# Small matmuls of a chunked recurrent attention laid out as 64x64 tiles in all four places of the array

## The chip, the core and the metric

The kernel runs on one NeuronCore of a Trainium2 chip. A core has five engines that run side by side and meet at semaphores: TensorE (PE) multiplies matrices and writes the results to PSUM; VectorE (DVE), ScalarE (ACT) and GpSimd (POOL) work element by element; SyncE (SP) issues transfers. PSUM has 8 banks of 512 float32 values in each of 128 partitions. The metric is the device time of one execution, in microseconds (us).

## What is computed

An attention with a recurrent state goes through 768 time steps for 4 batches of 8 heads with 40 channels. Its output feeds a mixture of experts with 8 experts.

```python
for t in range(S):
    y[:, :, t] = np.einsum('bhd,bhde->bhe', rt, state)
    Sa = np.einsum('bhde,bhe->bhd', state, at)
    state_decay = state * wt[:, :, None, :] - np.einsum('bhd,bhe->bhde', Sa, bt)
    state = state_decay + np.einsum('bhd,bhe->bhde', vt, kt)
...
for e in range(E):
    h = np.maximum(x @ w1[e], 0.0)
    ye = h @ w2[e]
    out += P[:, e:e + 1] * ye
```

`P` is a gate that is normalized over rows and columns in eight rounds.

## The kernel before

The attention is computed in 12 chunks of 64 time steps (`NCH`, `C`). A chunk is a batch of matrix products, and only a 40x40 state per head passes from chunk to chunk. The 8 heads of a batch are held as 4 pairs (`NP`): the first head of a pair lies on partitions 0 to 39, the second on 64 to 103 (`R2` = 104 partitions in all). Three functions write down the work:

- `prep(c, b)` prepares chunk `c` of batch `b`. It scales the inputs on DVE and POOL (`ab` at L310 is one product per head of the pair, each into its own half of a 128-column tile). `mm_ll` (L325, called `ll` below) multiplies all keys with `ab`, 4 matmuls of 128x128; `mm_kt` (L330, `kt`) transposes. ACT copies the results into a "set" of operands: `SX`, and `BB` (`bb` below).
- `merge(c)` completes the inverse of a triangular 64x64 matrix for each of the 32 heads of a chunk from 16x16 blocks, which DVE has inverted in `inverse`. Its matmuls are small: `mm_ga` (L427), `mm_at` (L433), `mm_tb` (L440, two calls with 32 matmuls each that stream 64 columns: a 32-column block with a block of zeros in front of or behind it), `mm_gb` (L448), `mm_tc` (L455).
- `step(c, b)` is the chain from state to state. `mm_av` (L518, `av`: 4 matmuls of 104x128) is masked by DVE into `f` (L521). `mm_xc` (L529, `xc`: two calls with 4 matmuls each, stationary operand 104 columns) gives `x` in rows 0 to 63 and `c1` in rows 64 to 103 of the same bank; ACT copies both parts of both halves (L534, L536). `mm_pu` (L543, `pu`) multiplies `x` with the inverse, 8 matmuls of 64x64 in two places: rows 0 to 63 into partitions 0 to 63, rows 64 to 127 into 64 to 127. DVE masks it (L546). `mm_c2` (L553, `c2`) is laid out in the same way. DVE adds `c1` to it and gives `ws` (L556). From `ws` come the output `y` (L583, POOL) and the new state `z` (L561, on POOL in chunks 0 to 8, then on DVE), which is transposed (`zt`, L569) for the next chunk. `mm_lp` (L598, `lp`) adds the gate's logits, once per two batches.

All matmuls of this part are in float32; each shows as two rows in the profile, the transposes as one.

The order is not the program's: each operation is put into a `Plan` with an engine, a length, what it depends on, a due time and the buffers that it takes and frees (`Token`). `order()` (L56) replays these lengths and writes the instructions of PE, DVE, ACT, POOL and SP in the order in which they start there. Each engine then runs its list strictly in order. `PACE` (7.5 us a step) sets the due times, `SIZES` the number of buffers; a PSUM token is one of 8 banks.

## Time and profile before

| | us |
|---|---|
| runs of the kernel before: median (lowest, highest) of 3 | 1875.62 (1865.92, 1876.19) |
| the profiled execution: its own time | 1871.58 |
| its span | 1869.6 |
| first to last `pu` matmul (the 48 steps) | 78.4 to 506.2 |
| last matmul of the attention ends, experts begin | about 511 |

The attention is the first quarter of the span and the experts the rest. In the views below a row names an engine, the line of the code, the operation, and the tiles in the form out<-in; `bk` is a PSUM bank. PEld is PE's weight load, which overlaps the matmuls. "issue" as a releaser means that the engine waited for nothing that the profile shows. PEclk is the share of PE's full clock that was granted.

### The profile page before, as it was taken

How to read it: one execution, taken by the hardware profiler on the slowest of the kernel's cores; microseconds unless marked ns; L12 is line 12 of the kernel's file. 1: busy time of each engine (PE TensorE's matmuls, PEld its weight loads, DVE VectorE, ACT ScalarE, POOL GpSimd, SP SyncE). 2: the span in 40 equal slices, each digit the busy share in tenths (PEclk: the TensorE clock that was granted, in tenths of full speed). 3: DMA queues.
4: the chain of work that ended last, by engine and by line, in shares of the span. 5: the costliest groups of instructions: out<-in, count | busy, mean ns of one | idle time of the engine just before them, and what ended most of it. 6: DMA issues, size and time to landing. Idle time of an engine off the chain costs nothing.

```text
span 1869.6 us, 41964 instructions
## 1 busy us (share of the span) xinstructions
PE 1761.5 (94%) x17219; PEld 1715.8 (92%) x17219; DVE 1311.6 (70%) x2278; ACT 877.1 (47%) x1900; POOL 870.7 (47%) x929
## 2 busy tenths in 40 slices
PE   5889999899849999999999999999999999999999
PEld 4778888888738899999999999999999999999999
DVE  8757557364378877686777767886776867767676
ACT  6757667665444434343343434344343434434342
POOL 7645545441175337182653718005371835538170
PEclk9789999888969999999999999999999999999999
DMA  8657666553332111020111102211110201111011
GB/s 184 146 112 153 134 137 150 122 115 72 87 99 60 37 37 56 19 74 19 56 38 38 55 19 74 60 29 38 37 57 18 74 19 56 39 36 65 11 37 43
DMA packets 189572, 126.70 MB, mean 68 GB/s; under 512 B 152261, under 2 KB 169285, under 8 KB 189381
## 3 DMA queue, kind: packets, MB, share of 16 engines
q1 hardware_dynamic: 188901, 123.53, 25.7%
q8 instruction: 135, 2.21, 0.5%
q10 hardware_dynamic: 480, 0.49, 0.1%
q14 instruction: 56, 0.46, 0.1%
HBM read 106.69 MB, written 17.30 MB: 66 GB/s over the span
## 4 chain that ended last, share of the span: by engine, by line
PE 86%; DVE 7%; issue 2%; DMA 2%; ACT 2%; SPq 0%; POOL 0%; DVEq 0%; ACTq 0%
PE op L827 35%; PE p L762 32%; PE bk L529 4%; PE bk L325 2%; PE bk L518 2%; PE bk L543 2%; PE bk L553 2%; PE bk L440 1%; PE bk L455 1%; PE bk L427 1%; PE bk L598 1%; DVE sm L780 1%; DMA xs<-xd 1%; PE bk L448 1%; PE bk L569 1%
## 5 line engine op out<-in xcount | busy, mean ns | idle before, releaser
L762 PE MATMUL p<-xch,wh 128*128 128x384 f32 (+1 forms) x1792 | 605.3, 339 | 30.9 <-ACT xch L736 22.6
L783 ACT ACTIVATE hh<-sm 128x384 fp32r<-128x384 f32 x512 | 269.3, 527 | 722.1 <-DVE sm L780 722.0
L827 PE MATMUL op<-wh,hh 128*128 128x320 f32 x1536 | 477.5, 311 | 2.2 <-ACT hh L783 2.0
L827 PE MATMUL op<-wl,hh 128*128 128x320 f32 x1536 | 475.1, 310 | 0.0
L827 PE MATMUL op<-wh,hl 128*128 128x320 f32 x1536 | 467.3, 310 | 0.3 <-DVE hl L786 0.3
L708 POOL TENSOR_TENSOR wl<-ws,wh 128x640 fp32r<-128x640 f32 x60 | 102.9, 1716 | 605.8 <-ACT wh L706 605.5
L786 DVE SCALAR_TENSOR_TENSOR hl<-sm,hh 128x384 fp32r<-128x384 f32 x512 | 372.4, 761 | 3.2 <-ACT hh L783 2.9
L762 PEld LDWEIGHTS p<-xch,wh 128*128 128x128 f32 (+1 forms) x1792 | 337.5, 188 | 36.2 <-ACT xch L736 22.7
L762 PE MATMUL p<-xcl,wh 128*128 128x384 f32 x896 | 302.8, 338 | 0.6 <-DVE xcl L742 0.6
L762 PE MATMUL p<-xch,wl 128*128 128x384 f32 x896 | 301.9, 337 | 0.0
L827 PEld LDWEIGHTS op<-wh,hh 128*128 128x128 f32 x1536 | 290.4, 189 | 3.6 <-ACT hh L783 3.6
L827 PEld LDWEIGHTS op<-wl,hh 128*128 128x128 f32 x1536 | 291.3, 190 | 0.0
L827 PEld LDWEIGHTS op<-wh,hl 128*128 128x128 f32 x1536 | 287.2, 188 | 0.6 <-DVE hl L786 0.5
L780 DVE TENSOR_TENSOR sm<-p,u 128x384 f32<-128x384 f32 x384 | 235.2, 623 | 8.7
L762 PEld LDWEIGHTS p<-xcl,wh 128*128 128x128 f32 x896 | 168.8, 188 | 1.1 <-DVE xcl L742 1.1
L762 PEld LDWEIGHTS p<-xch,wl 128*128 128x128 f32 x896 | 168.8, 188 | 0.0
L780 DVE TENSOR_TENSOR sm<-p,p 128x384 f32<-128x384 f32 x128 | 71.3, 557 | 129.7 <-PE p L762 75.0
L780 DVE TENSOR_TENSOR p<-p,p 128x384 f32<-128x384 f32 x128 | 71.2, 556 | 102.0 <-PE p L762 101.7
L780 DVE TENSOR_TENSOR u<-p,p 128x384 f32<-128x384 f32 x128 | 70.8, 553 | 58.5 <-PE p L762 57.3
L716 POOL TENSOR_TENSOR wl<-ss,wh 128x512 fp32r<-128x512 f32 x60 | 90.5, 1508 | 35.8 <-ACT wh L713 31.6
L583 POOL TENSOR_TENSOR y<-ws,st 104x256 f32<-104x256 f32 x48 | 39.7, 828 | 122.3 <-DVE ws L556 115.8
L891 DVE SCALAR_TENSOR_TENSOR acc<-op,pmat,acc 128x320 f32<-128x320 f32 x168 | 91.3, 544 | 4.5 <-PE op L827 4.4
(144 smaller groups left out, 2717.8 us busy)
## 6 DMA issues: line engine op xcount, KB each, us to landing
ws<-in_wts_dram SPq DMA_DIRECT2D x60, 832.0 KB
inp<-in_inp_dram SPq DMA_DIRECT2D x48, 450.2 KB
rb<-in_r_dram SPq DMA_DIRECT2D x48, 224.0 KB
ld<-lf SPq DMA_DIRECT2D x48, 128.0 KB
vz<-in_v_dram SPq DMA_DIRECT2D x48, 112.0 KB
f<-in_vt_dram SPq DMA_DIRECT2D x48, 80.0 KB
xd<-y SPq DMA_DIRECT2D x48, 80.0 KB
out_dram<-acc SPq DMA_DIRECT2D x42, 80.0 KB
```

Of the source, the lines that this page charges most:

```text
L325: nc.tensor.matmul(LL()[:, p].rearrange("s h t -> s (h t)"), lhsT=KB()[:, p].rearrange("r k t -> r (k t)"), rhs=AB()[:, p], start=True, st ...
L518: nc.tensor.matmul(AV()[:, p].rearrange("r h t -> r (h t)"), lhsT=VZ()[:, p], rhs=RB()[:, p], start=True, stop=True)
L529: nc.tensor.matmul(wide(b_xc[h])[0:R2, p], lhsT=pp["SX"]()[:, p, h], rhs=F()[:, p, h], start=True, stop=True)
L583: yy.append(P.add("POOL", 0.78, lambda: G.tensor_tensor(out=Y()[0:R2, :, b % 2], in0=WS()[:, :, 0:64], in1=pp["GF"]()[0:R2, :, 64:0:-1], o ...
L708: g.tensor_tensor(out=wl[:, 0:640], in0=raw[:, 256:896], in1=wh[:, 0:640], op=ALU.subtract)
L716: g.tensor_tensor(out=lv[:, 3:7], in0=so[:, :, 0], in1=hv[:, 3:7, 0], op=ALU.subtract)
L762: nc.tensor.matmul(o, lhsT=w_, rhs=x_, start=(j == 0), stop=(j == 3))
L780: eng.tensor_tensor(out=out, in0=x, in1=y, op=ALU.add)
L783: nc.scalar.activation(out=hh[:, f, h], in_=sm[f][:, h], func=AF.Relu)
L786: v.scalar_tensor_tensor(out=hl[:, f, h], in0=sm[f][:, h], scalar=0.0, in1=hh[:, f, h], op0=ALU.max, op1=ALU.subtract)
L827: nc.tensor.matmul(ops[i], lhsT=a[:, h, cs], rhs=w_[:, cw], start=(f == 0 and h == 0 and j == 0), stop=(last and h == 1 and j == 2))
L891: nc.vector.scalar_tensor_tensor(out=acc[:, m], in0=ops[i], scalar=pmat[:, n, e:e + 1], in1=acc[:, m], op0=ALU.mult, op1=ALU.add)
```

## The change

The attention's small matmuls are laid out anew, and the experts' code is untouched.

- PSUM tiles become pairs of banks. A token may take one bank or an aligned pair (`n=2`).
- `ll` and `av` become 16 matmuls of 64x64: the first or second head's rows (row group `h`) times the first or second half of the columns (`k`), in the order of `PLACES`, so that all four 64x64 places of the array are used in turn. Results of row group `h` go to bank `h` of a pair.
- `pu` and `c2` keep 8 matmuls of 64x64 and use four places, row group and column group varying against each other, a bank per row group.
- `xc` is split: `mm_x` gives only `x`, into partitions 0 to 63 for the first head and 64 to 127 for the second, so one ACT copy of 128 partitions takes it out. `mm_c1` gives `c1` into the pair of banks in which `c2` then adds to it (`start=False`). The copies of `c1` and the addition on DVE go.
- `ws` is an ACT copy of 64 columns per head, and `z` is taken by DVE straight from PSUM, in all chunks. The pair is held until both have read it.
- `tb` streams 32 columns in one call of 64 matmuls. ACT writes it out twice: multiplied by a 0/1 column `even` into `tt`, and whole into `r32`, which `tc` streams.
- `ab` is one product for both heads, `r` is loaded without its zero halves (half the bytes), sets go from 15 to 17, `PACE` from 7.5 to 6.0, and the lengths that the plan works with are set anew.

```diff
+    def grab(self, acq):
+            if tok.n == 2:
+                fit = [i for i in f if i % 2 == 0 and i + 1 in f]
+            else:
+                fit = tok.res == "ps" and [i for i in f if i ^ 1 not in f] or f
...
-    bank = many(ps, SZ["ps"], [128, 512], "bk")
+    pair = many(ps, SZ["ps"] // 2, [128, 2, 512], "bk")
...
         def mm_ll():
             for p in range(NP):
-                nc.tensor.matmul(LL()[:, p].rearrange("s h t -> s (h t)"), lhsT=KB()[:, p].rearrange("r k t -> r (k t)"),
-                                 rhs=AB()[:, p], start=True, stop=True)
+                for h, k in PLACES:
+                    nc.tensor.matmul(LL()[halves[k], h, p], lhsT=KB()[halves[h], p, k], rhs=AB()[halves[h], p],
+                                     start=True, stop=True)
...
-        def mm_tb(i):
-            for g in range(8):
-                for k, r in enumerate(quarter):
-                    x = 64 * (i * 8 + g) + (0 if k % 2 else 32)
-                    nc.tensor.matmul(B(b_tb[i], 8, 64)[r, g], lhsT=gt16[r, i * 8 + g], rhs=d16[r, x:x + 64],
-                                     start=True, stop=True)
+        def mm_tb():
+            for g in range(16):
+                for r in quarter:
+                    nc.tensor.matmul(B(b_tb, 16, 32)[r, g], lhsT=gt16[r, g], rhs=d16[r, g], start=True, stop=True)
...
         def mm_av():
             for p in range(NP):
-                nc.tensor.matmul(AV()[:, p].rearrange("r h t -> r (h t)"), lhsT=VZ()[:, p], rhs=RB()[:, p],
-                                 start=True, stop=True)
+                for h, k in PLACES:
+                    x = (slice(0, 64), slice(64, R2))[k]
+                    nc.tensor.matmul(AV()[x, h, p], lhsT=VZ()[halves[h], p, x], rhs=RB()[halves[h], p],
+                                     start=True, stop=True)
...
-                    nc.tensor.matmul(wide(b_xc[h])[0:R2, p], lhsT=pp["SX"]()[:, p, h], rhs=F()[:, p, h],
+        def mm_x():
+            for p in range(NP):
+                for h in range(2):
+                    nc.tensor.matmul(X()[halves[h], p ^ h], lhsT=pp["SX"]()[:, p, h, 0:64], rhs=F()[:, p, h],
                                      start=True, stop=True)
+        def mm_c1():
+            for p in range(NP):
+                for h in range(2):
+                    o = (2 * p + h) * 104 + 64
+                    nc.tensor.matmul(CP()[halves[h], p % 2, p // 2], lhsT=pp["ST"]()[:, o:o + 64], rhs=F()[:, p, h],
+                                     start=p < 2, stop=False)
+        p2 = P.add("PE", 0.74, mm_x, [v1, s0, l_t] + pp["sx"], acq=[b_x, t_x1], rel=[t_f])
+        ax = P.add("ACT", 0.52, lambda: A.copy(out=X1(), in_=X()), [p2], rel=[b_x])
+        pc = P.add("PE", 0.74, mm_c1, [p2] + pp["bb"], acq=[b_c], rel=[t_f])
...
         def mm_pu():
-            for p in range(NP):
-                for h in halves:
-                    nc.tensor.matmul(wide(b_pu)[h, p], lhsT=tt_b[t_tt.slot][h, b * NP + p], rhs=X1()[h, p],
-                                     start=True, stop=True)
+            for a in range(NP):
+                for h in range(2):
+                    nc.tensor.matmul(PU()[halves[(h + a) % 2], h, a // 2], lhsT=tt_b[t_tt.slot][halves[h], b * NP + (a ^ h)],
+                                     rhs=X1()[halves[h], a], start=True, stop=True)
...
         def mm_c2():
-            for p in range(NP):
-                for h in halves:
-                    nc.tensor.matmul(wide(b_c2)[h, p], lhsT=pp["BB"]()[h, p * 40:p * 40 + 64], rhs=PM()[h, p],
-                                     start=True, stop=True)
+            for a in range(NP):
+                for h in range(2):
+                    e, o = (h + a) % 2, (a // 2 * 2 + h) * 40
+                    nc.tensor.matmul(CP()[halves[h], e, a // 2], lhsT=pp["BB"]()[halves[e], o:o + 64],
+                                     rhs=PM()[halves[e], h, a // 2], start=False, stop=a > 1)
-        p4 = P.add("PE", 0.74, mm_c2, [v2] + pp["bb"], acq=[b_c2, t_ws], rel=[t_pm, pp["set"]])
-        v3 = P.add("DVE", 0.6, lambda: V.tensor_tensor(out=WS(), in0=wide(b_c2)[0:R2], in1=C1(), op=ALU.add),
-                   [p4] + ac, due, rel=[b_c2, t_c1])
+        p4 = P.add("PE", 0.46, mm_c2, [v2, pc] + pp["bb"], acq=[t_ws], rel=[t_pm, pp["set"]])
+        v3 = P.add("ACT", 0.4, lambda: A.copy(out=by_bank(WS()), in_=CP()[0:R2, :, :, 0:64]), [p4], due + 6, rel=[b_c])
...
-PACE = 7.5
+PACE = 6.0
+PLACES = ((0, 0), (1, 1), (0, 1), (1, 0))
```

The change also moves instructions, since the plan is replayed with new lengths and buffers. Three places show it. The first is PE between two merges, in the middle of the steps. Before, a stretch of it reads as follows; a row is a line, the operation, the tiles out<-in, columns of the output by columns streamed, and the count of matmuls (`f` is the operand of `xc`, `rb` of `av`, `ab` of `ll`, `x1` of `pu`, `pm` of `c2`, `z` of `zt`, and `cst` with `kb` that of `kt`).

```order
L553 MATMUL bk4_83<-pm0_130,st1_102 64x104 x8
L529 MATMUL bk1_80<-f2_125,st2_103 104x104 x4
L529 MATMUL bk0_79<-f2_125,st2_103 104x104 x4
L518 MATMUL bk3_82<-rb0_121,vz4_120 104x128 x4
L325 MATMUL bk4_83<-ab1_97,kb1_95 128x128 x4
L543 MATMUL bk1_80<-x10_126,tt1_142 64x104 x8
L569 MATMUL bk0_79<-cst_78,z0_136 40x104 x4
L330 MATMUL bk6_85<-cst_78,kb1_95 128x104 x4
```

The same engine in the changed program, in a like place (L538 is `x`, L545 `c1`, L555 `pu`, L566 `c2`, L338 `ll`, L581 `zt`, L343 `kt`, L610 `lp`):

```order
L338 MATMUL bk3_82<-ab0_92,kb0_90 64x64 x16
L610 MATMUL bk1_80<-gs_65,y0_130 128x8 x4
L581 MATMUL bk1_80<-cst_78,z0_132 40x104 x4
L555 MATMUL bk0_79<-x10_124,tt0_137 64x104 x8
L538 MATMUL bk1_80<-f1_122,st13_110 64x104 x8
L338 MATMUL bk3_82<-ab1_93,kb1_91 64x64 x16
L566 MATMUL bk2_81<-pm0_126,st12_109 64x104 x8
L545 MATMUL bk0_79<-f1_122,st13_110 64x104 x8
L555 MATMUL bk1_80<-x11_125,tt0_137 64x104 x8
L343 MATMUL bk2_81<-cst_78,kb1_91 128x104 x4
L581 MATMUL bk2_81<-cst_78,z1_133 40x104 x4
L566 MATMUL bk0_79<-pm0_126,st13_110 64x104 x8
```

`x` and `c1` of one step no longer stand side by side: groups of other steps are put between them. A `ll` is 16 matmuls where it was 4.

The second place is PE in a merge. Before, the two halves of `tb` (L440) and `tc` (L455) have groups of steps between them:

```order
L569 MATMUL bk1_80<-cst_78,z0_136 40x104 x4
L553 MATMUL bk2_81<-pm0_130,st0_101 64x104 x8
L330 MATMUL bk0_79<-cst_78,kb0_94 128x104 x4
L440 MATMUL bk1_80<-d16_149,g16_145 32x64 x32
L518 MATMUL bk3_82<-rb0_121,vz2_118 104x128 x4
L598 MATMUL bk0_79<-gs_65,y0_134 128x8 x4
L455 MATMUL bk1_80<-tt1_142,g32_146 64x32 x32
```

In the changed program `at` (L443) and the whole of `tb` (L449) stand close together, with 16 matmuls of `c2` and `pu` between them:

```order
L610 MATMUL bk2_81<-gs_65,y1_131 128x8 x4
L555 MATMUL bk1_80<-x10_124,tt0_137 64x104 x8
L538 MATMUL bk2_81<-f0_121,st0_97 64x104 x8
L443 MATMUL bk2_81<-g16_141,d16_145 32x32 x32
L566 MATMUL bk0_79<-pm0_126,st14_111 64x104 x8
L555 MATMUL bk1_80<-x11_125,tt0_137 64x104 x8
L449 MATMUL bk2_81<-d16_145,g16_141 32x32 x64
```

`tb` is one run of 64 matmuls where it was two of 32.

The third place is ACT, which PE's `pu` waits for. Before, a step takes four copies out of the two banks of `xc` (L534 `x`, L536 `c1`), and the copies of the prepared operands follow (L337 and L352), with those of the state (L512, L513, L574, L575):

```order
L534 COPY x10_126<-bk1_80 64x416
L536 COPY c11_129<-bk1_80 40x416
L534 COPY x10_126<-bk2_81 64x416
L536 COPY c11_129<-bk2_81 40x416
L337 ACTIVATE lf2_100<-bk3_82 64x256 x2
L512 COPY f0_123<-z0_136 40x4x40
L513 COPY f0_123<-z0_136 40x4x40
```

In the changed program it is one copy for `x` (L548), and the copy of `ws` (L569) stands between others:

```order
L548 COPY x11_125<-bk0_79 128x416
L569 COPY ws0_128<-bk1_80 104x2x2x64
L407 COPY tnd_152<-un_147 128x256
L586 COPY vz3_117<-bk0_79 40x4x40
L587 COPY vz3_117<-bk0_79 40x4x40
L569 COPY ws0_128<-bk1_80 104x2x2x64
```

The four copies have become one, and a `ws` copy, which was an addition on DVE, now stands in ACT's order.

More of the change, by code (lines that the diff above doesn't have):

```diff
@@ L222, in attention, with one, two @@
     halves = [slice(64 * h, 64 * h + 64) for h in range(2)]
+    def one(tok):
+        return pair[tok.slot // 2][:, tok.slot % 2]
+    def two(tok):
+        return pair[tok.slot // 2]
     def clear(eng, e, dur, t, v=0.0, deps=()):
@@ L593, in step @@
             b_lp = Token("ps")
-            LP = lambda: bank[b_lp.slot][:, 0:E]
+            LP = lambda: one(b_lp)[:, 0:E]
             def mm_lp():
```

223 lines of the change are left out of this document (102 added, 121 removed).

## The prediction

> **What bounds the kernel now.** There is one core, so the first thing read is the windows of its span. The attention stage runs up to about 508 us; behind it stands the mixture of experts, whose code the change leaves alone.
>
> ```profile
> core 0: us, PE busy (x) PEld busy (x) DVE busy (x) ACT busy (x) POOL busy (x), PEclk, DMA share, GB/s
> 800.00:1200.00 400.00, 400.00 (x2515) 399.74 (x2514) 302.32 (x512) 163.41 (x320) 203.26 (x176) 1.00 0.15 48
> 78.40:506.20 427.80, 394.61 (x8301) 361.86 (x8300) 240.74 (x443) 275.52 (x694) 177.81 (x282) 0.92 0.56 120
> ```
>
> In the back part PE is busy all the time at full clock. I carry its 1364 us over unchanged. The second row goes from the first `pu` matmul to the last, so it holds the 48 steps (12 chunks of 4): 427.8 us, or **35.65 us a chunk**. No engine but PE is near full there, and PE's granted clock is only 0.92 on average. Next, whom PE waits for:
>
> ```profile
> engine line waited for: us in total, times, longest us
> PE bk L448 <- issue: 8.8, 6, 2.2
> PE bk L427 <- issue: 6.9, 4, 2.8
> PE bk L440 <- issue: 5.1, 4, 2.2
> PE bk L553 <- DVE pm L546: 4.4, 1, 4.4
> PE bk L433 <- issue: 2.1, 3, 1.1
> ```
>
> This is the window 100 to 500 us. PE hardly waits for data (one wait of 4.4 us). It waits 22.9 us for "issue", always in the merge (L427 to L448). So PE's own work sets the pace, and something in its instruction supply adds to it. Its work, row by row at full clock, from the timeline (start, length, group; the next row's start minus this one's is what a group holds PE for):
>
> ```profile
> 395.64 1.08 PE L325 MATMUL bk<-ab,kb 128*128 128x128 f32 x8
> 396.56 1.04 PE L518 MATMUL bk<-rb,vz 128*104 128x128 f32 x8
> 397.52 0.93 PE L543 MATMUL bk<-x,tt 64*64 64x104 f32 x16
> 398.38 0.54 PE L569 MATMUL bk<-cst,z 104*40 104x104 f32 x4
> 398.76 0.52 PE L330 MATMUL bk<-cst,kb 104*128 104x104 f32 x4
> 399.11 1.08 PE L325 MATMUL bk<-ab,kb 128*128 128x128 f32 x8
> 400.12 0.93 PE L553 MATMUL bk<-pm,st 64*64 64x104 f32 x16
> 400.98 1.12 PE L518 MATMUL bk<-rb,vz 128*104 128x128 f32 x8
> 401.94 1.63 PE L529 MATMUL bk<-f,st 128*104 128x104 f32 x16
> 403.40 0.98 PE L598 MATMUL bk<-gs,y 104*128 104x8 f32 x8
> ```
>
> `ll` (L325) holds PE 0.92 us ahead of another whole-array group and 1.01 us ahead of a 64x64 one: a change of tile shape costs 0.09 us. Net of that, `av` (L518) is 0.87, `xc` (L529) 1.46, `pu` (L543) and `c2` (L553) 0.77 each, `zt` 0.38, `kt` 0.35; half an `lp` is some 0.42. Each matmul in the code is two rows here, except the transposes.
>
> **The supply.** The page gives PE's rows and the packets that bring instructions:
>
> ```profile
> PE 1761.5 (94%) x17219; PEld 1715.8 (92%) x17219; DVE 1311.6 (70%) x2278; ACT 877.1 (47%) x1900; POOL 870.7 (47%) x929
> q8 instruction: 135, 2.21, 0.5%
> ```
>
> 34,438 rows of PE over 135 packets is 255: one packet holds 256 PE instructions (a matmul row and its weight load are two). A merge shows what happens when they are used up faster than they come:
>
> ```profile
> 417.06 0.25 PE L427 MATMUL bk<-a,l 32*32 32x32 f32 x5 [1.16 <-issue]
> 419.03 0.72 PE L433 MATMUL bk<-g,d 32*32 32x32 f32 x62
> 419.57 0.19 PE L433 MATMUL bk<-g,d 32*32 32x32 f32 x1
> 421.00 0.53 PE L440 MATMUL bk<-d,g 32*32 32x64 f32 x22 [0.59 <-issue]
> 421.46 0.24 PE L448 MATMUL bk<-a,lf 32*64 32x32 f32 x1
> 422.52 0.85 PE L440 MATMUL bk<-d,g 32*32 32x64 f32 x42
> 424.83 0.53 PE L440 MATMUL bk<-d,g 32*32 32x64 f32 x22 [1.46 <-issue]
> 429.13 0.74 PE L427 MATMUL bk<-a,l 32*32 32x32 f32 x36 [1.32 <-issue]
> 435.18 1.91 PE L325 MATMUL bk<-ab,kb 128*128 128x128 f32 x8
> 437.02 1.14 PE L543 MATMUL bk<-x,tt 64*64 64x104 f32 x16
> ```
>
> PE starts again after "issue" at 417.06, 421.00, 424.83 and 429.13: 3.94, 3.83 and 4.30 us apart, **4.0 us a packet**. No packet follows faster in this stretch, whatever is in it. And the stalls cost clock behind them:
>
> ```profile
> 427.30:437.50 10.20, 8.88 (x162) 8.39 (x150) 1.06 (x2) 1.61 (x4) 0.00 (x0) 0.50 0.16 31
> ```
>
> For 10.2 us the clock is halved, and `ll` at 435.18 takes 1.84 us for its 0.92. A mean of 0.92 over 427.8 us is 68 us at half clock, 5.7 us a chunk.
>
> **The change part by part.**
>
> *`ll` and `av`* go from 4 matmuls to 16 of 64x64 (32 rows, four at a time). The nearest row is `gb` (L448): four tiles at a time, 64 columns of weights, 64 rows from 421.46 to 422.52, 1.06 us. So 32 rows take 0.53 us for 0.92 and 0.87: -0.39 and -0.34.
>
> *`pu` and `c2`* keep their 16 rows but may run four at a time instead of two: 0.77 halves to 0.39, twice -0.38.
>
> *`xc`* becomes `x` and `c1`, 128x64 tiles, two side by side, 16 rows each: priced like `pu` today, 0.77 each, 1.54 for 1.46, +0.08.
>
> That column tiles of one row group run side by side is carried by `at` (L433). Its matmuls use row groups 0 and 2 only, with two column groups each; 62 rows start within 0.54 us, 8.7 ns apiece. `ga` below uses four row groups at 8.8 ns. The Trainium skill (TensorE: Matmul & The Clock Gate, "The mechanism") says that a weight load overlaps matmuls in flight only where the row group differs; by it the column tiles would follow one another, and rival E has what that gives. The 8.7 ns disagree.
>
> *The merge's `tb`* is now two calls (L440) of 64 rows that stream 64 columns, and becomes one of 128 rows that stream 32, the shape of `ga` (L427).
>
> ```profile
> 446.36 1.09 PE L440 MATMUL bk<-d,g 32*32 32x64 f32 x64
> 447.39 0.93 PE L553 MATMUL bk<-pm,st 64*64 64x104 f32 x16
> 474.12 1.29 PE L427 MATMUL bk<-a,l 32*32 32x32 f32 x128
> 475.34 1.71 PE L529 MATMUL bk<-f,st 128*104 128x104 f32 x16
> ```
>
> Twice 1.03-0.09 is 1.88; `ga` takes 1.22-0.09, 1.13: -0.75 a merge. `gb` and `tc` keep count and shape: nothing.
>
> *Tile shapes* change more often: counted along PE's order in the attention, 251 times before and 296 now, +45 x 0.09 = +4 us.
>
> Sum of PE's work: 48 x (-0.39-0.34-0.38-0.38+0.08) = -68, 12 x (-0.75) = -9, +4: **-73 us**. Twelve of the `ll` lie ahead of the first `pu`, where PE waits for its inputs, so 5 us of it are worth nothing: -68 us, 5.7 a chunk.
>
> *The instructions* go the other way. A step issued 152 (`ll` 16, `kt` 8, `av` 16, `xc` 32, `pu` 32, `c2` 32, `zt` 8, `lp` 8) and now issues 280 (`ll` and `av` 64 each, `x` and `c1` 32 each). A merge stays at 896. A chunk goes from 1504 to 2016, from 5.9 packets to **7.9**, and at 4.0 us each these need 31.5 us. PE's own work in a chunk was 35.65 less 2.0 of stalls (22.9 us over nearly 12 merges) and less what the halved clock costs. From the rows: four steps of 5.94 and some 0.3 of shape changes, 25.0; a merge of 6.4 (`ga` 1.13, `at` 0.54, `tb` 1.88, `gb` 0.97, `tc` 1.9, an estimate from its 64 rows at twice `gb`'s spacing) and 0.5 of changes: 31.9. That leaves 1.75 for the clock. Now it is 31.9-6.1, 25.8 us: **less than the packets need**. That is the step that eats most of the gain.
>
> How much? If the merge's 3.5 packets took 4.0 each (14.0) and the steps' 4.4 packets their work (4 x 4.9 = 19.6), it would be 33.6 us. If work and packets overlapped perfectly, 31.5. The order puts two or three step groups between a merge's parts, so neither; I take 32.8, a little above the middle, because `at`, `tb` and `gb` (512 instructions, two packets) often stand together. On top comes the clock: 1.75 us today from 5.7 us at half clock. More packets stall, so I take 1.95. That makes 34.75 us a chunk, -0.9 x 12 = -11 us.
>
> On that last term: the row at 427.30 shows a halved clock behind waits of 1.46 and 1.32 us. The Trainium skill (TensorE: Matmul & The Clock Gate, "HAM oscillation — how this bites in real kernels") says that only gaps of PE above some 3.4 us bring the clock down; the longest wait for issue here is 2.8 us, so by it the 1.95 would be nothing, which is rival B. The row disagrees.
>
> *Other engines.*
>
> ```profile
> L536 ACT COPY c<-bk 40x416 f32<-40x416 f32 x96 | 48.2, 502 | 2.0
> L556 DVE TENSOR_TENSOR ws<-bk,c 104x416 f32<-104x416 f32 x47 | 27.7, 590 | 31.4 <-PE bk L553 22.7 <-ACT vz L575 2.6 <-POOL l L408 1.9
> L561 POOL TENSOR_TENSOR z<-ws,st 104x160 f32<-104x160 f32 x36 | 17.3, 486 | 0.5
> L310 POOL TENSOR_TENSOR ab<-inp,st 40x256 f32<-40x256 f32 x88 | 67.4, 766 | 20.5 <-DVE st L289 9.6 <-ACT lf L337 6.8 <-ACT st L352 0.2
> ```
>
> ACT loses both `c1` copies and one of two equally long `x` copies (3 x 0.50) and gains the `ws` copy, whose 256 columns I price between L536's 0.50 for 416 and their share of it, 0.31: -1.0 to -1.2 us a step of 5.7. DVE loses the `ws` add (0.59) and takes POOL's 36 `z` products (0.49): -11 us in all. POOL loses these and 48 of 88 `ab` products: -54 us. All three sit beside PE and stay free: worth nothing here. Where cover is gone: behind the new `ws` copy on ACT wait the `x` copies of the next step, for which `pu` waits; ACT had 152 us idle in the window. `c1` now waits for the prepared `bb`, as only `c2` did, with `pu` of the next step behind it on PE; it is prepared chunks ahead. The state's path gets shorter by L556's 0.59 us, and in four interleaved batches nobody waits for it. Pairs of banks are a new resource: `c1`'s pair is held until both `ws` and `z` are read. PE shows no wait for a bank today; I price it between 0 and one wait as long as the longest data wait, 4.4 us, and take 0. On the SP queue only `r` shrinks by half. In the opening POOL drops 8 products of 0.77: 6 us if they sat on the path, nothing if not; I take 0.
>
> The sum is made against the profiled execution, 1871.58 us (span 1869.6): 1871.6-11 = **1861 us**, 0.8% below the median of the runs, 1875.62, of which the profiled one lies 4 us short.
>
> **The rivals.**
>
> *A (forecast), packets and clock eat most of it:* 1861, by itself 1849 to 1874. Chance 0.35.
>
> *B, the clock does not suffer.* Without any cost of the clock a chunk is 32.8 us, -2.85 x 12 = -34: **1837 us**. Against it stands the halved clock behind waits of 1.46 and 1.32 us; for it, that the stretch shown stands behind a merge, where packets and not the clock set the pace. Chance 0.24.
>
> *C, packets come in time* because the merge's bursts are spread between steps: PE's work sets the end, -68: **1804 us**. Against it: 4.0 us in each interval above. Chance 0.13.
>
> *D, slower: the clock stays low.* PE has less work per packet, so it idles more, and the halved clock lasts longer. A chunk of 32.8 reaches today's 35.65 when the clock costs 2.85 us, at today's rate (1.75 for 5.7) 9.3 us at half clock a chunk, a granted clock of 0.87. At 16 us (granted 0.79) it costs 4.9: 37.7 us, +2.05 x 12 = +25: **1896 us**. Chance 0.20.
>
> *E, column tiles of one row group do not run side by side.* Then `x` and `c1` take 1.46 each, `pu` and `c2` stay at 0.77, `ll` and `av` need 1.06: 6.6 for 4.79, +1.8 x 48 = +87 us, less 5 for `tb` and changes: **1953 us**. `at`'s 8.7 ns speak against it. Chance 0.04.
>
> *F, only the row groups fail to pair:* PE's work falls by little and packets fill the rest, near 1875. Chance 0.04.
>
> **How the numbers follow.** The likeliest is A, 1861. B, C and D reach on both sides; leaving out half of C, half of D's upper side and E gives 1806 to 1898. One per cent is 1856.9 to 1894.4, about what a measurement of this kernel tells from no change. Faster: B, C and a fifth of A, 0.44. Slower: E and most of D, 0.19. The same: 0.37.
>
> **What would show it.** In the window from first to last `pu`: length 34.7 us a chunk, granted clock about 0.90. Packets of q8 in the attention: 94 for 70 (12 chunks by the counts above). "Issue" waits of PE far above 23 us, now also in `ll` and `av`. `ll` and `av` near 0.53 us, `pu` and `c2` near 0.39, `x` and `c1` near 0.77 in the timeline. Wrong it is if "issue" stays near 23 us (C), if the clock stays at 0.92 or more while PE waits (B), if it falls under 0.87 (D), or if data or banks come to lead PE's waits.

## The result, and the profile after

The changed kernel takes 1933.49 us (median of 4 runs, 1928.41 to 1937.29) for 1875.90 us before (4 runs, 1865.92 to 1879.58): a ratio of **1.0314, 95% interval 1.0264 to 1.0364**. It is slower by 58 us, where 1861 us were forecast, 11 us less than the profiled execution before; it lies above the range.

First the windows of the changed kernel's span, 1935.3 us (us, busy time and count of each engine, PEclk, DMA share, GB/s): the opening up to the first `pu`, from the first `pu` to the last, and a part of the experts.

```profile
0.00:88.40 88.40, 45.67 (x1116) 38.39 (x1116) 58.88 (x113) 52.48 (x129) 41.35 (x85) 0.64 0.67 152
88.40:567.80 479.40, 392.73 (x10940) 341.89 (x10944) 212.66 (x422) 234.30 (x621) 133.40 (x240) 0.76 0.44 94
...
800.00:1200.00 400.00, 400.00 (x2514) 399.75 (x2513) 291.03 (x487) 158.25 (x310) 201.73 (x175) 1.00 0.12 41
```

Of the 65.7 us by which the profiled span grew, 51.6 lie in the 48 steps (479.4 us for 427.8), 10.0 ahead of them, and 4.1 behind them (1367.5 us for 1363.4). In the steps PE is busy as long as before, 392.7 us for 394.6, at a clock of 0.76 for 0.92, and idle for 86.7 us instead of 33.2. By the prediction's rows PE's work there is 12 x 25.8 = 310 us at full clock instead of 12 x 31.9 = 383. So: -73 us of work, +71 of busy time above it (83 for 12) through the halved clock, +53.5 of idle time. The granted clock gives the same size: 0.24 x 479.4 = 115 us of clock lost instead of 0.08 x 427.8 = 34, a part of it in idle time.

The work did shrink as priced. The timeline of PE (start, length, group, the wait ahead of it in brackets):

```profile
407.90 0.69 PE L338 MATMUL bk<-ab,kb 64*64 64x64 f32 x32 [0.28 <-ACT ws L569]
408.39 0.57 PE L566 MATMUL bk<-pm,st 64*64 64x104 f32 x16
...
422.90 1.22 PE L449 MATMUL bk<-d,g 32*32 32x32 f32 x120
426.76 0.26 PE L449 MATMUL bk<-d,g 32*32 32x32 f32 x8 [2.64 <-issue]
...
433.76 0.69 PE L527 MATMUL bk<-rb,vz 64*64 64x64 f32 x32
434.39 0.54 PE L581 MATMUL bk<-cst,z 104*40 104x104 f32 x4
...
444.36 0.94 PE L538 MATMUL bk<-f,st 128*64 128x104 f32 x16 [0.26 <-ACT st L360]
445.23 0.59 PE L566 MATMUL bk<-pm,st 64*64 64x104 f32 x16
...
448.10 0.59 PE L566 MATMUL bk<-pm,st 64*64 64x104 f32 x16
448.51 1.23 PE L527 MATMUL bk<-rb,vz 64*64 64x64 f32 x64
```

At full clock `ll` (L338) holds PE for 0.49 us (forecast 0.53), `av` (L527) 0.63 less one change of shape, 0.54 (0.53), `x` (L538) 0.87 less one, 0.78 (0.77), `c2` (L566) 0.41 (0.39). The packets are as counted too:

```profile
PE 1760.6 (91%) x20291; PEld 1693.2 (87%) x20291; DVE 1279.1 (66%) x2264; ACT 834.0 (43%) x1825; POOL 810.1 (42%) x877
...
q8 instruction: 159, 2.61, 0.6%
```

159 for 135, 24 more. Next PE's waits from the first `pu` to the last (us in total, times, longest):

```profile
PE bk L449 <- issue: 22.0, 11, 3.6
PE bk L437 <- issue: 7.8, 7, 1.9
PE bk L456 <- issue: 5.3, 4, 1.6
PE bk L566 <- DVE pm L558: 4.8, 3, 3.4
...
PE bk L555 <- DVE lg L613: 2.1, 1, 2.1
PE bk L343 <- ACT vz L587: 2.0, 4, 1.5
...
PE bk L338 <- ACT vz L587: 1.9, 2, 0.9
```

The first three are the merge's `tb`, `ga` and `gb`. All rows of this view together give 46.7 us for issue (before 23.7) and **40.5 us for ACT, DVE and POOL (before 8.5)**, in many small pieces. The largest, 4.8 us, is a wait for an input: `c2` reads `pm`. The last three rows are of the other kind: `pu` waits for the copy of the logits, `kt` and `ll` for the copy of the transposed state. These are not their inputs; PE waits for a bank. Stranger are the waits of the other engines, of which these are a few, ACT's first and then DVE's:

```profile
ACT vz L586 <- PE bk L343: 13.8, 8, 2.5
...
ACT tt L479 <- PE bk L343: 9.8, 2, 5.6
...
ACT st L360 <- PE bk L538: 9.7, 4, 2.7
```

```profile
DVE z L572 <- ACT ws L569: 29.2, 16, 9.1
DVE lg L613 <- PE bk L581: 19.2, 3, 16.5
```

The copy of the transposed state (L586) needs `zt`, yet it waits for `kt` (L343); the merge's copy (L479) needs `tc` and waits for `kt`; the copy of the logits (L613) needs `lp` and waits for `zt` (L581). None of these three reads what it waits for. Nor does `z` (L572): it and the copy of `ws` (L569) only read the same pair of banks, `z` on DVE and the copy on ACT, and one waits for the other.

### The profile page after: what moved, and what is told of

The parts are those of the page before. It is cut to its first block, busy times and chain, and to the rows that moved or that the text cites. A ratio compares the mean times of both kernels' runs of the same rounds, so it can differ in the third digit from the quotient of the medians.

```text
span 1935.3 us, 47802 instructions
## 1 busy us (share of the span) xinstructions
PE 1760.6 (91%) x20291; PEld 1693.2 (87%) x20291; DVE 1279.1 (66%) x2264; ACT 834.0 (43%) x1825; POOL 810.1 (42%) x877
## 4 chain that ended last, share of the span: by engine, by line
PE 81%; DVE 4%; ACT 3%; issue 3%; DMA 1%; SPq 0%; POOL 0%; DVEq 0%; ACTq 0%; POOLq 0%
PE op L839 34%; PE p L774 31%; PE bk L538 2%; PE bk L545 2%; PE bk L464 2%; PE bk L527 1%; PE bk L610 1%; PE bk L581 1%; PE bk L566 1%; PE bk L555 1%; PE bk L456 1%; PE bk L449 1%; PE bk L343 1%; DVE sm L792 1%; DMA xs<-xd 1%
## 5 line engine op out<-in xcount | busy, mean ns | idle before, releaser
L792 DVE TENSOR_TENSOR sm<-p,p 128x384 f32<-128x384 f32 x128 | 71.3, 557 | 132.0 <-PE p L774 78.3
```

The lines of the kernel that those rows point to most:

```text
L792: eng.tensor_tensor(out=out, in0=x, in1=y, op=ALU.add)
```

## The experiments

All runs in one table: the median, the ratio to the kernel before on the same chip, and, from the profile, the length from the first `pu` to the last, the clock there, and PE's waits there for issue and for everything else, which is ACT, DVE, POOL and at most 1.0 us of DMA (all rows of the view added up).

| run | us | ratio (95%) | first to last pu | clock | issue | others |
|---|---|---|---|---|---|---|
| before | 1875.90 | 1 | 427.8 | 0.92 | 23.7 | 8.5 |
| changed | 1933.49 | 1.0314 (1.0264, 1.0364) | 479.4 | 0.76 | 46.7 | 40.5 |
| e1_wide | 1981.15 | 1.0579 (1.0530, 1.0628) | 511.0 | 0.72 | 33.9 | 31.5 |
| e2_pace | 1943.19 | 1.0390 (1.0356, 1.0423) | 482.4 | 0.75 | 29.1 | 65.4 |
| e3_warm | 1939.13 | 1.0365 (1.0328, 1.0402) | 465.8 | 0.84 | 31.4 | 39.9 |
| e4_split | 1889.58 | 1.0096 (1.0068, 1.0125) | 441.8 | 0.91 | 27.5 | 7.0 |
| e5_few | 1836.59 | 0.9805 (0.9774, 0.9836) | 378.3 | 0.90 | 0.0 | 59.9 |
| e6_ps6 | 1954.79 | 1.0455 (1.0416, 1.0495) | 484.2 | 0.79 | 41.1 | 60.2 |
| e7_warm2 | 1953.10 | 1.0439 (1.0405, 1.0473) | 492.4 | 0.85 | 24.9 | 44.3 |
| e8_pu | 1952.67 | 1.0420 (1.0378, 1.0462) | 497.9 | 0.84 | 10.3 | 75.2 |
| e9_pairs | 1880.24 | 1.0033 (1.0002, 1.0063) | 438.7 | 0.90 | 30.1 | 9.1 |
| e13_pu_slow | 1974.08 | 1.0549 (1.0481, 1.0618) | 511.1 | 0.88 | 7.6 | 66.1 |
| e10_few_before | 1814.82 | 0.9690 (0.9633, 0.9747) | 378.2 | 0.96 | 0.2 | 13.6 |
| e11_spread | 1867.96 | 0.9994 (0.9965, 1.0022) | 426.6 | 0.93 | 14.5 | 10.0 |
| e14_tiles | 1964.77 | 1.0466 (1.0413, 1.0519) | 505.4 | 0.88 | 7.2 | 74.7 |
| e16_pu_banks | 1862.85 | 0.9941 (0.9907, 0.9975) | 417.0 | 0.90 | 29.2 | 14.5 |
| e15_banks | 1904.18 | 1.0171 (1.0093, 1.0248) | 452.5 | 0.80 | 58.4 | 22.1 |
| e17_few_banks | 1806.72 | 0.9656 (0.9617, 0.9695) | 357.2 | 0.88 | 0.3 | 35.7 |
| e18_pu_spread | 1850.32 | 0.9891 (0.9849, 0.9932) | 396.8 | 0.94 | 9.1 | 19.0 |
| e19_all_spread | 1915.88 | 1.0213 (1.0182, 1.0245) | 460.3 | 0.79 | 32.5 | 42.8 |

### First: instructions, the plan, or PE's shorter work

Three explanations stand against each other, and the expectations below give what each would show: PE runs short of instructions (the supply theory), PE has too little work between its data (little-work), or the order laid out for the new pace is at fault (plan). Fewer instructions in the changed kernel:

```diff
-                for h, k in PLACES:
-                    nc.tensor.matmul(LL()[halves[k], h, p], lhsT=KB()[halves[h], p, k], rhs=AB()[halves[h], p],
+                for h in range(2):
+                    nc.tensor.matmul(LL()[:, h, p], lhsT=KB()[halves[h], p].rearrange("r k t -> r (k t)"), rhs=AB()[halves[h], p],
                                      start=True, stop=True)
... (av in the same way)
```

> The changed kernel, with ll and av as 8 matmuls each of 64 rows by 128 (av: 104) columns instead of 16 of 64x64. Same results, same order of groups, same pairs of row groups; a step issues 216 instructions of PE instead of 280, a chunk 1760 instead of 2016 (6.9 packets of 256 instead of 7.9). Supply theory (PE runs out of instructions, and the clock falls behind these stalls): waits for issue fall from about 43 us to about 30, the granted clock between the first and the last pu rises from 0.76 to about 0.85, the time falls to about 1890 us. Little-work theory (the clock falls because PE has too little work between its data, whatever the instructions): granted clock stays at 0.76, the time within 1% of 1933 us. Plan theory (the order laid out for 6.0 us a step is at fault): no change either.

Measured 1981 us. The waits for issue fell to 33.9 us as the supply theory had it, but the clock went down, not up, and every theory missed the time. One reason is a price that none had worked out: 64x128 tiles take longer here than 64x64 ones. From the timeline of PE in this run, `av` (L526) and `ll` (L338):

```profile
405.67 0.95 PE L526 MATMUL bk<-rb,vz 64*104 64x64 f32 x16
406.45 1.06 PE L338 MATMUL bk<-ab,kb 64*128 64x64 f32 x16
...
443.21 1.11 PE L338 MATMUL bk<-ab,kb 64*128 64x64 f32 x16
444.25 1.43 PE L437 MATMUL bk<-a,l 32*32 32x32 f32 x128
```

`ll` holds PE for 1.04 less a change of shape, 0.95 us, where the 64x64 tiles took 0.49, and `av` for 0.78, where they took 0.54: (0.46 + 0.24) x 48 = 34 us more work. So the run does not test the supply alone.

The old pace, in the plan of the changed kernel:

```diff
-PACE = 6.0
+PACE = 7.5
```

> The changed kernel with PACE 7.5, as before the change, in place of 6.0; everything else is the changed kernel, only the plan's order differs. Plan theory: merges and steps stand apart again, the granted clock returns to about 0.9 and the time to about 1870 us. Supply theory: as many instructions, so within 1% of 1933 us. Little-work theory: within 1% of 1933 us.

1943 us, clock 0.75, where the plan theory had 1870 and 0.9: the pace is not the cause. Extra streaming in the merge of the changed kernel:

```diff
         def mm_tb():
+            for _ in range(2):
+                nc.tensor.matmul(one(b_tb), lhsT=gt16[:, 0:4].rearrange("r g x -> r (g x)"),
+                                 rhs=d16.rearrange("r g x -> r (g x)"), start=True, stop=True)
... (one such matmul at the head of mm_ga)
```

> The changed kernel with extra work: three matmuls of 128x128 that stream 512 columns in each merge, one ahead of ga and two ahead of tb, into the banks that ga and tb overwrite behind them. Estimated from x (L538, 8 rounds of 104 columns in 0.77 us at full clock) at 0.47 us a row, 2.8 us a merge, 34 us in all, with only 12 more PE instructions a merge. If PE's work set the time: +34 us, 1967 us. Supply theory and little-work theory both hold that these 34 us lie beside waits and lift the granted clock: no slower than 1933 us, granted clock above 0.76, between 1900 and 1933 us; supply theory adds that waits for issue at tb (L449, 22 us) fall by half or more.

1939 us: some 34 us of added PE work (an estimate) cost nothing that can be measured (the intervals of 1.0365 and 1.0314 overlap), the clock rose to 0.84, and the window shrank by 13.6 us, in the fastest of the four executions. So PE's work alone does not set the time of the changed kernel. Twice the dose went on too far:

```diff
-            for _ in range(2):
+            for _ in range(4):
                 nc.tensor.matmul(one(b_tb), lhsT=gt16[:, 0:4].rearrange("r g x -> r (g x)"),
... (two in mm_ga)
```

> The changed kernel with twice the extra streaming of the first such run: two matmuls of 128x128 over 512 columns ahead of ga and four ahead of tb, 5.6 us a merge, 68 us in all, as much PE work as the change took away. Streaming theory (the clock follows the share of time in which PE streams columns, and gaps cost more by the clock than by their length): the granted clock rises further, from 0.84 to about 0.90, and the time stays between 1915 and 1950 us although PE has 68 us more to do than in the changed kernel. If the first dose was only absorbed by waits for issue, of which 31 us are left in pieces elsewhere: clock at 0.84, time about 1970 us.

1953 us at a clock of 0.85: between the two cases. The first dose lay beside waits, the second mostly did not.

More instructions for the same streaming, in the kernel before:

```diff
-                nc.tensor.matmul(LL()[:, p].rearrange("s h t -> s (h t)"), lhsT=KB()[:, p].rearrange("r k t -> r (k t)"),
-                                 rhs=AB()[:, p], start=True, stop=True)
+                for q in quarter:
+                    nc.tensor.matmul(LL()[q, p].rearrange("s h t -> s (h t)"),
+                                     lhsT=KB()[:, p].rearrange("r k t -> r (k t)")[:, q], rhs=AB()[:, p], start=True, stop=True)
... (av in the same way)
```

> The kernel before, with ll and av as 16 matmuls each of 128 rows by 32 columns in place of 4 of 128x128, four column tiles side by side: the same streaming, but a step issues 248 PE instructions instead of 152, a chunk 1888 instead of 1504 (7.4 packets for 5.9). Supply theory: more stalls and a lower clock than 0.92, 1890 to 1920 us for 1876. Little-work and plan theory: PE's work is unchanged, so within 1% of 1876 us.

+1.0%, at the lower edge of what the supply theory had. The window grew by 14.0 us, but the waits for issue by only 3.8. Most of the rest is a busier PE:

```profile
79.20:521.00 441.80, 406.19 (x10210) 360.60 (x10207) 240.23 (x443) 275.53 (x693) 178.20 (x281) 0.91 0.53 116
```

406.2 us for 394.6, at a clock of 0.91 for 0.92 and with more changes of tile shape, as no group but these two has such tiles. So 1.5 packets more a chunk cost little here, while PE's own work is long.

### Second: which waits, and which part of the change

Few instructions in the merge of the changed kernel (the inverse's blocks are not computed):

```diff
         def mm_ga():
-            for g in range(16):
-                for r in quarter:
-                    nc.tensor.matmul(B(b_ga, 16, 32)[r, g], lhsT=lp16[r, g], rhs=at16[r, g], start=True, stop=True)
+            nc.tensor.matmul(one(b_ga), lhsT=ident, rhs=flat(at16, 16), start=True, stop=True)
... (at, tb and gb in the same way)
```

> The changed kernel, with the merge's ga, at, tb and gb each replaced by one or two matmuls of 128x128 that copy an operand into the same banks (512, 256, 512 and twice 256 columns): the blocks of the inverse are not computed, so the output differs. PE's time in a merge stays nearly the same (ga 0.9 for 1.13 us, at 0.45 for 0.54, tb 0.9 for 1.13, gb 0.9 for 0.97, by the 0.43 us for 512 columns of a row that x gives), a merge issues 148 PE instructions instead of 896, a chunk 5.0 packets instead of 7.9. Supply theory (the gaps are waits for instructions): waits for issue fall from 46.7 us to under 10, the clock rises from 0.76 to about 0.90, the time to about 1850 us. Bank theory (the gaps that matter are waits of PE for ACT and DVE to empty banks, 40.5 us): these stay at 40 us or more, the clock stays under 0.82, the time between 1890 and 1915 us.

1837 us, clock 0.90, no wait for issue. 748 instructions fewer a merge were worth 5% of the whole time, more than the supply theory asked. Yet the waits for the other engines rose to 59.9 us: two causes stand side by side. The same in the kernel before:

```diff
         def mm_ga():
...
+            nc.tensor.matmul(bank[b_ga.slot], lhsT=ident, rhs=flat(at16, 16), start=True, stop=True)
... (at, tb and gb in the same way)
```

> The kernel before, with the merge's ga, at, tb and gb replaced by one or two wide copying matmuls each, as was done to the changed kernel (1837 us); the inverse's blocks are not computed, so the output differs. PE's time in a merge is nearly the same, a chunk issues 756 PE instructions instead of 1504. Supply theory: the 23.7 us of waits for issue go and the clock rises from 0.92 to 0.96 or more: 1830 to 1845 us, so that with instructions in ample supply the two kernels would tie within 1%. If the change is worth its 73 us of PE work where instructions are no limit, this run must lie well above 1837 us: 1870 us or more.

1815 us, so the change does not even pay where instructions are no limit: 1837 against 1815. Something else holds it back. Fewer banks in the changed kernel's plan:

```diff
-             inv=1, m_a=1, m_d=1, m_l=1, m_m=1, m_g=1, m_t=1, m_h=1, m_r=1, ps=8)
+             inv=1, m_a=1, m_d=1, m_l=1, m_m=1, m_g=1, m_t=1, m_h=1, m_r=1, ps=6)
```

> The changed kernel with 6 PSUM banks in the plan (3 pairs) instead of 8 (4 pairs); the same instructions in another order. Bank theory: PE's waits for ACT, DVE and POOL rise from 40.5 us to 70 or more between the first and the last pu, and the time to 1960 to 1995 us. Supply theory: the number of instructions is the same, within 1% of 1933 us.

+1.4% on the changed kernel, waits for others 60.2 us: banks matter, less than the bank theory said. Three tiles of two banks instead of four also tie more operations to each other, so this run does not tell scarce banks from what comes below. One part of the change alone, in the kernel before (`bb`, `pm` and `ws` laid out for it, all else as before):

```diff
+    pair = many(ps, SZ["ps"] // 2, [128, 2, 512], "bk")
+    bank = [pair[i // 2][:, i % 2] for i in range(SZ["ps"])]
...
+        b_pu, b_c2 = (Token("ps", 1, 2) for _ in range(2))
...
-            for p in range(NP):
-                for h in halves:
-                    nc.tensor.matmul(wide(b_pu)[h, p], lhsT=tt_b[t_tt.slot][h, b * NP + p], rhs=X1()[h, p],
+            for a in range(NP):
+                for h in range(2):
+                    nc.tensor.matmul(PU()[halves[(h + a) % 2], h, a // 2], lhsT=tt_b[t_tt.slot][halves[h], b * NP + (a ^ h)],
+                                     rhs=X1()[halves[h], a ^ h], start=True, stop=True)
... (c2 in the same way)
```

> The kernel before with one part of the change alone: pu and c2 as 64x64 tiles in all four places, a pair of banks each (bb laid out for it by ACT, pm by DVE, ws still added by DVE); PACE, sets and everything else as before. PE has 2 x 0.38 x 48 = 36 us less to do and not one instruction more. If PE's work alone set the time: 1876 - 36 = 1840 us. Streaming theory: part of it goes to a lower clock (0.92 to about 0.88): 1850 to 1870 us. Bank theory: PE's waits for ACT and DVE rise from 7.5 us to 20 or more, and the time stays within 1% of 1876 us or rises.

This was the turn: 1953 us, **+4.2% from the one part that adds no instruction** and takes 36 us of work away. PE waits 75.2 us for the other engines and only 10.3 for issue. Is it the shorter PE, or the banks? With 36 us of PE work put back:

```diff
         def mm_pu():
+            nc.tensor.matmul(pair[b_pu.slot // 2][:, 0, 0:208], lhsT=ident, rhs=X1()[:, 0:2].rearrange("r p x -> r (p x)"),
+                             start=True, stop=True)
... (the like in mm_c2)
```

> The kernel before with pu and c2 in four places (which took 1953 us), order and banks unchanged, with one matmul of 128x128 over 208 columns put ahead of pu and one ahead of c2, into banks that these overwrite: 2 x 0.38 x 48 = 36 us of PE work back, and two changes of tile shape a step more. Slack theory: waits for ACT and DVE fall from 72 us and the granted clock rises from 0.84 to about 0.90, so that the time falls, to 1880 to 1920 us, though PE has 36 us more to do. Bank theory: the banks are held just as long or longer, so 1950 us or more.

1974 us: the slack theory falls. With pairs of banks taken in the plan, and nothing else:

```diff
-        b_av, b_pu, b_c2, b_zt = (Token("ps") for _ in range(4))
+        b_av, b_zt = (Token("ps") for _ in range(2))
+        b_pu, b_c2 = (Token("ps", 1, 2) for _ in range(2))
... (and the search for a free pair, as in the changed kernel)
```

> The kernel before, in which pu and c2 only take a pair of banks each in the plan and go on using the first bank of it, in two places as before: PE's work and instructions are those before, only banks are scarcer and the order of the plan shifts. Bank theory (pairs are what cost the run with pu and c2 in four places its 82 us): PE's waits for ACT and DVE well above 7.5 us, the time 1900 to 1950 us. Slack theory (PE's work set the pace and hid every other engine's lateness; a shorter PE has no slack, waits in order, and loses clock): 1865 to 1885 us, within 1% of before.

1880 us: scarcer banks are not it either. Besides the four places themselves, what this run leaves out of the one of 1953 us is the line that makes the banks: 4 tiles of two banks instead of 8 of one.

### Third: the tiles of two banks

```diff
-    bank = many(ps, SZ["ps"], [128, 512], "bk")
+    pair = many(ps, SZ["ps"] // 2, [128, 2, 512], "bk")
+    bank = [pair[i // 2][:, i % 2] for i in range(SZ["ps"])]
```

> The run in which pu and c2 only take pairs of banks in the plan (1880 us), with one edit: the 8 banks are made as 4 tiles of two banks instead of 8 tiles of one. Order, instructions and PE's work are the same. Coupling theory (an access to one bank of a tile waits for the users of the other bank): PE's waits for ACT and DVE rise from 9 us to 40 or more, the time to 1930 to 1970 us. Order theory and slack theory: no change, within 1% of 1880 us.

**1965 us for 1880, from this edit alone.** The plan is the same (the two traces show DVE, ACT and POOL with the attention's operations in the same order), every operation uses the same bank for the same data, and PE has the same work. Only which tile a bank belongs to has changed, and with it the waits that the program is built with. First DVE and ACT in the run with pairs in the plan and one-bank tiles:

```profile
DVE f L537 <- PE bk L534: 66.6, 23, 14.2
```

```profile
ACT tt L489 <- PE bk L470: 22.3, 9, 4.4
```

`f` waits for `av` and the merge's copy for `tc`, their inputs. Then in the run with tiles of two banks:

```profile
DVE f L538 <- ACT tt L482: 32.8, 4, 14.1
DVE f L538 <- PE bk L471: 17.9, 2, 15.8
DVE f L538 <- ACT tt L490: 16.8, 1, 16.8
```

```profile
ACT tt L490 <- PE bk L546: 12.2, 5, 3.2
...
ACT c L553 <- PE bk L341: 8.8, 8, 1.3
ACT tt L490 <- PE bk L341: 8.0, 2, 6.6
```

`f` waits up to 16.8 us for copies of the merge and for `tc` (L471), the merge's copy for `xc` (L546) and `ll` (L341), the copy of `c1` for `ll`. An access to one bank of a tile waits for users of the other bank: engines that had nothing to do with each other are chained, in the plan's order. PE's waits for the others go from 9.1 to 74.7 us. Order, banks and data are the same in both runs, so these waits come with the program as it is built. The long waits of the first run, DVE for PE, cost little, since PE had other work meanwhile; these reach PE.

Now `pu` and `c2` in four places on 8 tiles of one bank:

```diff
+        b_pu, b_c2 = ([Token("ps"), Token("ps")] for _ in range(2))
...
+        for h in range(2):
+            v2.append(P.add("DVE", 0.36, lambda h=h: V.tensor_tensor(
+                out=PM()[:, h], in0=PU(h), in1=mask_p.unsqueeze(1).broadcast_to([128, 2, 104]), op=ALU.mult),
+                [p3] + v2, rel=[b_pu[h]]))
... (ws in the same way, bank by bank)
```

> The kernel before with pu and c2 in four places (1953 us on tiles of two banks), now on 8 tiles of one bank: pm and ws are taken in two DVE products each, one per bank. Coupling theory: the 82 us are gone, PE's waits for ACT and DVE under 20 us; PE has 36 us less to do, of which the supply and the clock leave some: 1840 to 1870 us. Slack theory (a shorter PE in the plan lays the engines too tight): still 1900 us or more.

1863 us: the loss is gone, and this part of the change is a gain of 0.6%. The slack theory, which had 1900 us or more, fails here too. The whole change in the same way:

```diff
-    pair = many(ps, SZ["ps"] // 2, [128, 2, 512], "bk")
+    bank = many(ps, SZ["ps"], [128, 512], "bk")
...
-        b_av, b_pu, b_c = (Token("ps", k, 2) for k in (1, 1, 1 if c + 1 == NCH else 2))
+        b_av, b_pu, b_c = ([Token("ps", k), Token("ps", k)] for k in (1, 1, 1 if c + 1 == NCH else 2))
... (ll and gb too; DVE and ACT take each bank out by an operation of its own)
```

> The whole change on 8 tiles of one bank: ll, av, gb, pu and c2 take two single banks, and DVE and ACT take them out in two operations each. PE's instructions and work are those of the changed kernel. Coupling theory: PE's waits for ACT, DVE and POOL fall from 40.5 us to under 20, the clock rises; waits for issue stay at 40 us or more, as there are just as many instructions: 1860 to 1895 us. If the coupling is nothing: 1925 us or more.

1904 us: nearly half of the loss is gone, though 1860 to 1895 were expected. The edit also frees the banks from having to be neighbours and adds operations on DVE and ACT, so the difference is not the coupling's alone. Its window, and the head of PE's waits in it:

```profile
81.30:533.80 452.50, 370.97 (x10933) 324.66 (x10936) 228.69 (x602) 239.81 (x680) 136.95 (x242) 0.80 0.47 101
```

```profile
PE bk L442 <- issue: 21.7, 10, 3.0
PE bk L430 <- issue: 12.9, 8, 2.3
PE bk L436 <- issue: 8.2, 4, 3.1
```

The waits for the others fell from 40.5 to 22.1 us (under 20 were expected), and what leads now is the supply, in the merge's `tb`, `ga` and `at`: 58.4 us in all. The other 1.7% could be that. So, few instructions in its merge:

```diff
+            nc.tensor.matmul(one(b_ga), lhsT=ident, rhs=flat(at16, 16), start=True, stop=True)
... (at, tb and gb in the same way; the inverse's blocks are not computed)
```

> The whole change on one-bank tiles (1904 us), with the merge's ga, at, tb and gb replaced by wide copying matmuls as in the two earlier runs of that kind; the inverse's blocks are not computed, so the output differs. Supply theory: waits for issue go from 58 us to under 5, the granted clock from 0.80 to 0.90 or more, and the time falls below the 1815 us of the kernel before with the same merge, to 1780 to 1805 us: the change's saving of PE work is real once banks and instructions no longer stand against it. If something else holds it back (short tiles, the chain from state to state): 1815 us or more.

1807 us, just above the expected 1780 to 1805, and not to be told from the kernel before with the same merge (0.9656 and 0.9690, intervals that overlap). The windows show a gain that the whole does not keep: 357.2 us here and 378.2 there.

```profile
74.80:432.00 357.20, 320.81 (x6818) 258.96 (x6822) 226.25 (x600) 238.58 (x680) 137.64 (x240) 0.88 0.61 128
```

```profile
76.70:454.90 378.20, 363.55 (x4220) 313.03 (x4220) 247.74 (x443) 274.94 (x696) 181.08 (x283) 0.96 0.61 134
```

43 us less busy PE gives 21 us, at a clock of 0.88 for 0.96. Behind the last `pu`, 1371.0 us follow here (span 1803.0) and 1362.1 there (span 1817.0); the runs of this document have 1362 to 1372. Some of these 9 us are clock at the start of the experts, 0.57 in the first 48 us and 0.88 in the next 40 for 0.64 and 0.96; what sets it there stays open.

### Fourth: the merge spread between the steps

```diff
+    def spread(dur, fn, n, k, deps, acq=(), rel=()):
+        o = None
+        for i in range(k):
+            o = P.add("PE", dur / k, lambda i=i: fn(range(n * i // k, n * i // k + n // k)), deps if o is None else [x],
+                      acq=[] if i else acq, rel=rel if i + 1 == k else [])
+            if i + 1 < k:
+                x = P.add("GAP", 0.6, lambda: None, [o])
+        return o
...
-        p1 = P.add("PE", 1.35, mm_ga, la + lx, acq=[b_ga, t_g], rel=[t_a, t_m])
+        p1 = spread(1.35, mm_ga, 16, 4, la + lx, acq=[b_ga, t_g], rel=[t_a, t_m])
... (at, tb and gb in the same way)
```

> The kernel before, with ga put into the order in four pieces, at, gb and both calls of tb in two pieces each, with at least 0.9 us between pieces in the plan so that groups of the steps come between them; the same instructions, spread. Supply theory: waits for issue fall from 23.7 us to under 10 and the clock rises from 0.92 to about 0.95: 1840 to 1860 us. If spreading makes the merge late for its steps or costs tile shape changes instead (some 8 more a merge at 0.09 us, 9 us): 1875 to 1890 us.

In the kernel before: no difference, where the supply theory had 1840 to 1860, though the waits for issue fell to 14.5 us. PE was busy for 401.7 us instead of 394.6; the pieces bring more changes of tile shape, which the second theory names. On `pu` and `c2` in four places with one-bank tiles the same edit does help:

> The kernel before with pu and c2 in four places on one-bank tiles (1863 us), with the merge's groups put into the order in pieces, as in the earlier run that spread them. Supply theory: waits for issue fall from 29 us to under 18, the clock rises from 0.90, the time to 1840 to 1855 us. If spreading takes as much as it gives, as it did alone (1868 us for 1869): 1855 to 1870 us.

**1850 us, 1.1% faster than the kernel before** (0.9891, interval 0.9849 to 0.9932), as the supply theory expected, with 9.1 us of waits for issue, and the fastest of the kernels that compute everything:

```profile
79.80:476.60 396.80, 368.05 (x8301) 326.46 (x8304) 248.34 (x535) 273.84 (x692) 177.68 (x280) 0.94 0.58 128
```

On the whole change with one-bank tiles it does not:

> The whole change on one-bank tiles (1904 us) with the merge's ga and tb put into the order in four pieces each, at and gb in two, with groups of the steps between them. Supply theory: a chunk still needs 7.9 packets, 31.5 us at 4.0 us each, so waits for issue fall from 58 us but not under 25, the clock rises from 0.80 to about 0.87, the time to 1860 to 1885 us. If the placing of the merge alone were at fault: under 1850 us, as with few instructions of PE's own.

1916 us, a miss for both. The waits for issue fell to 32.5 us as expected, but those for the others rose to 42.8, and the clock stayed at 0.79. What these later pieces hold up was not followed further, so it stays open whether another order could bring the whole change below the kernel before.

## Why the prediction was wrong

*The step that failed* is the one on the pairs of banks: "I price it between 0 and one wait as long as the longest data wait, 4.4 us, and take 0." It looked at how long a pair is held and not at what a tile of two banks ties together. The runs put 85 us on that in the kernel before (1880 to 1965 us with the same plan) and, in the whole change, the distance from 1.0314 to 1.0171, some 27 us net of the added operations on DVE and ACT. It also moves the opening, which was taken at 0: the first `pu` came at 88.4 us for 78.4, and on one-bank tiles at 81.3. Of the 62 us by which the window missed its forecast (479.4 for 34.75 x 12 = 417), 27 go with the two-bank tiles (479.4 to 452.5). The other 35 remain on one-bank tiles, and the next paragraph takes them apart.

*The clock's term* was mis-sized: 1.95 us a chunk, at a clock of 0.90. Its start, 1.75, was only what the sum left over: 2.0 us of waits for issue were taken off, but PE idled for 33.2 us in the window, 2.8 a chunk. Without the coupling the changed kernel takes 452.5 / 12 = 37.7 us a chunk at a granted clock of 0.80. By the prediction's rows that is 25.8 of work, 5.1 of busy time above it (371.0 - 310), 4.9 of waits for issue and 1.8 of waits for other engines: 5.1 stands where the forecast had 1.95. (In the whole change it is 83 / 12 = 6.9.) The 37.7 us at 0.80 are rival D nearly to the figure, which had 37.7 us at 0.79, and 1896 us for the measured 1904. Part of this is luck, as D had 7.0 us for packets (32.8 - 25.8) where 4.9 were measured, and nothing for other engines. Even without the pairs D and not A was the case. D's reason held, that PE idles more: 81.5 us without the coupling, 33.2 before. The packets themselves cost less than A gave them, and the halved clock more.

*Right* were the prices of the matmuls, within 0.04 us each in the rows shown, and with them PE's 73 us; the 24 packets; and waits for issue "far above 23": 46.7 us, now also in `av` (3.7 us). Rivals B (the clock does not suffer) and C (packets come in time) fall with the 0.76 and the 46.7 us. Rival E falls by `x`: 0.78 us. The Trainium skill (TensorE: Matmul & The Clock Gate, "The mechanism") would have these column tiles of one row group follow one another; the row disagrees. F falls by `ll` and `c2`.

*The clock's cause.* Of all waits of PE in the steps of the changed kernel two are longer than 3 us, 3.6 for issue and 3.4 for `pm`, and the clock is 0.76. The Trainium skill gives a gap of some 3.4 us as the limit for one idle stretch (TensorE: Matmul & The Clock Gate, "HAM oscillation — how this bites in real kernels"), but right behind it, in "A second HAM failure mode: psum-queue depth-cycling", tells of a kernel in which frequent short idle times of PE had the same effect. This trace agrees with the second, and the prediction had weighed only the first. No run was made to test what brings the clock down; the last section has what the traces say of it.

## What to carry to other kernels

Before pricing a new layout of PSUM at nothing, look at which waits the program is built with: a tile over two banks is one thing to whoever sets the waits, and each of its banks inherits the other's users. A saving on TensorE was paid here only as far as its instructions arrived and its data were there; the rest came back as idle time and a lower clock. The part that saves work and adds no instructions (`pu` and `c2`) gained; whether `ll` and `av`, which save as much with four times as many, lose by themselves was not run. Time the parts one at a time: a part worth 0.6% stood here inside a change that lost 3.1%.

## What the runs showed of the hardware

For `ll`, tiles of 64x128 gained nothing: it took 0.95 us in 16 rows of them, for 0.92 in 8 rows of 128x128 and 0.49 in 32 rows of 64x64.

The clock does not simply follow PE's idle time. The run with 64x128 tiles waited less than the changed kernel (65.4 us of waits for 87.2) and was granted less, 0.72 for 0.76; the run with wide matmuls in the merge waited 71.3 us and was granted 0.84. Both added some 34 us to PE, the one in the merges with 512 columns streamed for one set of weights, the other in the steps with 64.

The clock records of all 20 runs tell more. They know only full and half clock and change in stretches of 3.41 us. Let a matmul row stream for 0.9 ns a column at full clock and for twice that at half (an estimate from `ll` before, 0.92 us for 8 rows of 128 columns), and take the stretches between 60 and 600 us. Of the 211 at full clock in which columns stream for less than 40% of the time, 206 are followed by half clock; of the 1454 with 60% or more, 10. Of the 292 at half clock with 85% or more, 272 are followed by full clock; of the 582 with less than 75%, 3. PE's busy time tells less: of 413 stretches at full clock with PE busy for less than 70%, 247 are followed by half clock. In the steps of the kernel before, 10 of 105 stretches at full clock stream for less than 45%; in the changed kernel 22 of 72. So the clock of these runs goes with the streaming in the stretch before. That is a reading of the traces and not a test: no run was made for it, and whether it accounts for the 0.72 and the 0.84 above was not worked out.
